# One stride per load of x, a first chunk reordered, and the tables split 17 and 10: a change to the head of a fused FFT and channel-mix kernel

## The chip, the cores and the metric

The kernel runs on one core of a Trainium2 chip. The metric is the time on the device in microseconds (us). The kernel before took 457.84 us (median of three runs, 457.7 to 458.09). A profile shows a "span" that is about 1.8 us shorter than the time of the same run. A difference of less than 2% counts as "same"; this whole study is about tenths of a per cent, so most comparisons were timed in five rounds beside the kernel before on the same chip. A gain or a loss against the kernel before is spoken of where the 95% interval of the ratio leaves out 1.

## The reference

```python
X = np.fft.fft(x, axis=1); X = np.fft.fft(X, axis=2); x = X.real   # x: (8, 3072, 256)
x_prev = concat([zeros, x[:, :-1]], axis=1)
xk = mu_k * x + (1 - mu_k) * x_prev
xr = mu_r * x + (1 - mu_r) * x_prev
k = np.maximum(xk @ w_k, 0)          # 256 -> 1024
v = k * k @ w_v                      # 1024 -> 256
r = 1 / (1 + np.exp(-(xr @ w_r)))    # 256 -> 256
return r * v
```

So each of the 8 batches goes through a two-dimensional Fourier transform (real part) and then through three projections with a squared relu and a sigmoid gate.

## The kernel before

The transform is done by matmuls in stages: `a_sum` or `a_item` (48 points along the sequence, on 96 partitions), `d_item` (along the model dimension, into `g_all`), `c_item` (64 points along the sequence, with tables `m1` and `m2` of 27 "slots", into `pq`). Then VectorE forms halves, differences and mixes, and TensorE does the projections of 48 chunks, in a list of steps. Each step has one `k_piece` (a quarter of a chunk's first projection), one `v_tile` of an earlier chunk, and whatever is registered for that step with `at`. The results of matmuls stand in PSUM, and ScalarE (ACT) or VectorE (DVE) copies them out, which is called evacuating. A gather is a DMA on GpSimd (POOL) that fetches rows by a list of indices; x is the input and `mu` the mixing weights. The parts that matter here:

```python
def load_part(b, h, n, q0, nq):            # x of one batch, on two times 48 partitions
    for g in range(2):
        r0 = 32 * g + 16 * h + q0
        nc.gpsimd.dma_start(out=xh_t[b, h][48 * g:48 * g + 48, q0:q0 + nq],
                            in_=x_r[b, :, r0:r0 + nq, :])
...
NS1 = 9                                    # slots in the first part of the tables
...
def loads():                               # all issued on GpSimd
    ...                                    # gathers of wk[0], mu
    load_xh(1, 0)
    ...                                    # gathers of wr[0], load of wv
    load_xh(1, 1)
    ...                                    # gathers of wk[1], wr[1]: not needed before step 12
...
def mirrored_mu():                         # mu for the mirrored half, first used at step 8
    for a in range(2):
        V.tensor_copy(out=mu_m[:, a], in_=mu_f[:, 1 - a])
    V.tensor_copy(out=mu_m[0:1], in_=mu_f[0:1])
...
at(0, m_rest, 1)                           # special slots 25 and 26, on VectorE
at(5, plain_128)                           # tables for the later batches, on VectorE
at(7, mirrored_mu)
at(8, mix, 0, 0, 1, 0)                     # reads mu_m
```

Of the kernel before, what the change touches and what calls it, by code (L numbers as in the profile page):

```python
# [35 lines left out]
def kernel(  # L36
# [14 lines left out]
    P = 128  # L51
# [3 lines left out]
    NS1 = 9  # L55
# [42 lines left out]
    x_r = x.rearrange("b (n1 r) d -> b n1 r d", r=R)  # L98
# [3 lines left out]
    def load_part(b, h, n, q0, nq):  # L102

        for g in range(2):
            r0 = 32 * g + 16 * h + q0
            nc.gpsimd.dma_start(out=xh_t[b, h][48 * g:48 * g + 48, q0:q0 + nq],  # L106
                                in_=x_r[b, :, r0:r0 + nq, :])

    def load_xh(b, h):
        xh_t[b, h] = xh_pool.tile([96, 16, 256], FP16, name="xh")  # L110
        load_part(b, h, 1, 0, 16)
# [36 lines left out]
    load_part(0, 0, 2, 0, 8)  # L148
# [4 lines left out]
    load_part(0, 0, 2, 8, 8)  # L153
# [5 lines left out]
    load_part(0, 1, 2, 0, 8)  # L159
    load_part(0, 1, 2, 8, 4)  # L160
    load_part(0, 1, 2, 12, 4)
# [21 lines left out]
    def g_zeros(u0, u1):  # L183
# [8 lines left out]
    hi48 = const.tile([P, 1], FP32)  # L192
# [14 lines left out]
    V.tensor_scalar(out=hi48, in0=pcol_f, scalar1=48.0, scalar2=None, op0=ALU.is_ge)  # L207
    V.tensor_scalar(out=n1f, in0=hi48, scalar1=-48.0, scalar2=pcol_f,
# [4 lines left out]
                    scalar2=1.0 / N1, op0=ALU.mult, op1=ALU.mult)  # L213
# [6 lines left out]
    for g in range(2):  # L220
        for n in range(2):
            V.tensor_scalar(out=w_sg[:, n, g:g + 1], in0=hi48, scalar1=2.0 * g - 1.0,
                            scalar2=1.0 - g, op0=ALU.mult, op1=ALU.add)
        V.tensor_scalar(out=w_sg[:, 2, g:g + 1], in0=hi48, scalar1=1.0 - 2.0 * g,
                        scalar2=g - 1.0, op0=ALU.mult, op1=ALU.add)
# [72 lines left out]
    def m_rest(part):  # L298



        s = 26 if part else 0
        if part:
            V.tensor_scalar(out=m2[hi64, 25], in0=m1[hi64, 25], scalar1=-1.0, scalar2=None,
                            op0=ALU.mult)
            V.tensor_copy(out=m1[hi64, 25], in_=m1[lo64, 25])
        for n, m in enumerate((m1, m2)):
            V.tensor_scalar(out=m[hi64, s], in0=m[hi64, s], scalar1=-1.0, scalar2=None,
                            op0=ALU.mult)
            if part:  # L310
                V.memset(m[lo64, 25], 0.0)
            else:
                V.tensor_copy(out=mz[lo64, n], in_=m[lo64, 1])
                V.memset(m[:, 0, 0:1], 0.0)
# [11 lines left out]

    g_zeros(13, 24)
# [8 lines left out]
    def loads():  # L336

        V.memset(mu_f, 0.0)
        mus = [mu.rearrange("(a b) -> a b", b=1) for mu in (moe_mu_k, moe_mu_r)]
        for i, mu in enumerate(mus):  # L340
            nc.sync.dma_start(out=mu_f[0:1, 0, i:i + 1], in_=mu[0:1])
            nc.sync.dma_start(out=mu_f[1:65, 0, i:i + 1], in_=mu[1:129:2][0:64])
            nc.sync.dma_start(out=mu_f[65:128, 0, i:i + 1], in_=mu[2:128:2])
        for a in range(2):
            gather(wk_sb[0][a], moe_w_k, a)
        for i, mu in enumerate(mus):
            gather(mu_f[:, 1, i:i + 1], mu, 1)
        load_xh(1, 0)
        for a in range(2):
            gather(wr_sb[0][a], moe_w_r, a)  # L350
        nc.gpsimd.dma_start(out=wv_sb, in_=moe_w_v.rearrange("(fc p) v -> p fc v", p=128))
        load_xh(1, 1)
        for a in range(2):
            gather(wk_sb[1][a], moe_w_k, 2 + a)
        for a in range(2):
            gather(wr_sb[1][a], moe_w_r, 2 + a)
# [12 lines left out]
    def plain_128():  # L369

        V.memset(w_eo[:, 0, 63:64], 1.0)
        V.tensor_scalar(out=w_eo[:, 0, 127:128], in0=w_eo[:, 0, 127:128], scalar1=-2.0,
                        scalar2=1.0, op0=ALU.mult, op1=ALU.add)
        V.memset(u128, 0.0)

        V.tensor_copy(out=tw[lo64, 0, 1:NSL], in_=m1[lo64, 1:NSL, 0])
        V.tensor_copy(out=tw[hi64, 0, 1:NSL], in_=m2[hi64, 1:NSL, 0])
        V.tensor_copy(out=tw[hi64, 1, 1:NSL], in_=m1[hi64, 1:NSL, 0])
        V.tensor_scalar(out=tw[lo64, 1, 1:NSL], in0=m2[lo64, 1:NSL, 0], scalar1=-1.0,
                        scalar2=None, op0=ALU.mult)  # L380
        V.memset(tw[hi64, :, 1:2], 0.0)

        for n, half, sign in ((0, lo64, 1.0), (0, hi64, -1.0), (1, lo64, -1.0), (1, hi64, 1.0)):
            V.tensor_scalar(out=tw[half, n, 0:1], in0=tw[half, n, 2:3], scalar1=sign,
                            scalar2=None, op0=ALU.mult)
# [55 lines left out]
    def d_half(b, u, ps, eng):  # L441
        d_units(b, ps, u, 2)
        evac(g_all[:, u:u + 2, 1:257],
             ps[:, 0:512].rearrange("p (i c) -> p i c", c=256), eng)

# [81 lines left out]
    def mix_short(b, lo, hi):  # L527

        x_t[b, 0, 0] = xo = x_t.get((b, 0, 0)) or mix_pool.tile([P, 2, 1536], FP16, name="x00")
        for a in range(2):  # L530
            V.scalar_tensor_tensor(out=xo[:, a, 64 * lo:64 * hi],
                                   in0=_v(x_t[b], 64 * (26 * a + lo), [(1, 64 * (hi - lo))]),
                                   scalar=mu_f[:, a, 0:1],
                                   in1=_v(y_t[b], 64 * (NSL * a + lo), [(1, 64 * (hi - lo))]),
                                   op0=ALU.mult, op1=ALU.add)
# [4 lines left out]

    def mix2(b, j, m, lo, hi):
        for a in range(2):
            mix(b, j, m, a, lo, hi)
# [41 lines left out]
    def v_tile(c, tb):  # L585

        apart = c == chunks[-1] and tb >= 2
        h = 0 if apart else tb % 2
        if h == 0:
            st["v"] = ps_v()  # L590
        for fc in range(8):
            nc.tensor.matmul(out=st["v"][:, 256 * h:256 * h + 256],  # L592
                             lhsT=k2_t[c][:, fc, 128 * tb:128 * tb + 128],
                             rhs=wv_sb[:, fc], start=(fc == 0), stop=(fc == 7))

    def v_out(c, tb, n):
# [6 lines left out]
                               in0=st["v"][:, 0:256 * n], scalar=16.0,  # L603
# [17 lines left out]
    m_rest(0)  # L621
    loads()
    m_angles(NS1, NSL)
# [8 lines left out]
    m_wrap(NS1, NSL)  # L632
# [7 lines left out]
    d_item(0, 2)  # L640
    m_sine(NS1, NSL)
    d_item(0, 3)
    for lo, hi in ((0, 4), (4, 8)):
        halves(0, lo + (lo > 0), hi + 1)
        diff(0, lo, hi)
        mix_short(0, lo, hi)
# [5 lines left out]
    def at(step, f, *args):  # L652
        work.setdefault((step, "x" if f in (a_item, a_sum, d_item, c_item, r_item) else "w"),
                        []).append((f, args))

    def mirrored_mu():

        for a in range(2):
            V.tensor_copy(out=mu_m[:, a], in_=mu_f[:, 1 - a])
        V.tensor_copy(out=mu_m[0:1], in_=mu_f[0:1])  # L660

    chunks = [(b, m, i) for b in range(B) for m in range(2) for i in range(3)]
    nk = 4 * len(chunks)
    LAG = 5
    keep_busy(4)
    k_products(chunks[0], 0, 0, 256)
    k_products(chunks[0], 1, 0, 256)
    d_half(0, 16, ps_v(), "A")
    d_half(0, 18, ps_v(), "A")
    for n, c in enumerate(chunks):  # L670
        at(4 * n + (5 if n in (0, 2) else 4), r_item, c)


    at(0, m_swap, NS1, NSL)
    at(0, m_rest, 1)
    at(0, mix2, 0, 1, 0, 0, 8)
    at(1, c_item, 0, 9, 8)
    at(1, halves, 0, 9, 17)
    at(1, diff, 0, 8, 16)
    at(1, mix2, 0, 0, 0, 8, 16)  # L680
    at(2, d_item, 0, 5)
    at(2, a_sum, 1, 0, 0)
    at(3, c_item, 0, 17, 8)
    at(5, butterfly, 1, 1, 0)
    at(4, halves, 0, 17, 25)
    at(4, diff, 0, 16, 24)
    at(5, a_sum, 1, 0, 4)
    at(5, a_sum, 1, 0, 8)
    at(5, mix2, 0, 0, 0, 16, 24)
    at(6, a_sum, 1, 0, 12)  # L690
    at(6, c_item, 0, 25, 2)
    at(6, load_xh, 2, 0)
    at(6, mix2, 0, 1, 0, 8, 16)
    at(7, butterfly, 1, 1, 1)
    at(7, halves, 0, 25, 27)
    at(7, diff, 0, 24, 26)
    at(7, mirrored_mu)
    at(7, load_xh, 2, 1)
    at(8, mix, 0, 0, 1, 0)
    at(9, mix, 0, 0, 1, 1)  # L700
    at(10, mix2, 0, 1, 0, 16, 24)
    at(12, mix, 0, 1, 1, 0)
    at(14, mix, 0, 1, 1, 1)
    for n, st0 in enumerate((7, 8, 9, 10)):
        at(st0, a_item, 1, 1, n // 2, n % 2, "A")
    at(5, plain_128)
    for n, st0 in enumerate((12, 13, 13, 14, 15, 17)):
        at(st0, d_item, 1, n)
    at(18, turned, 1)
    for n, st0 in enumerate((14, 15, 18, 19)):  # L710
        at(st0, c_item, 1, (0, 7, 14, 21)[n], 7 if n < 3 else 6)

    for b in range(B):
# [8 lines left out]
        if t < B:  # L722
            for n, st0 in enumerate((9, 10, 12, 14) if b else (11, 13, 15, 24)):
# [9 lines left out]
        if t < B:  # L733
            at(s0 + 16, halves, t, 0, 14)
# [13 lines left out]
    for step in range(nk + LAG):  # L748
# [3 lines left out]
        vs = step - LAG  # L752
        if vs >= 0:
            v_tile(chunks[vs // 4], vs % 4)
        due(step, "w")
        if vs >= nk - 2:
            v_out(chunks[vs // 4], vs % 4, 1)
        elif vs >= 0 and vs % 2:
            v_out(chunks[vs // 4], vs % 4, 2)
# [34 lines left out]
```

## Time and profile before

The profile that the prediction quotes further down was of a run of 461.26 us. In a timeline of TensorE (PE) the columns are start, busy time, engine, line, operation, output from inputs, shape, count, and in brackets the idle time before the group with what ended it.

```profile
9.46 1.48 PE L421 MATMUL psW<-w_pm,xh 96*128 96x192 f16 x16 [1.44 <-DMA xh<-in_x_dram]
...
19.43 0.27 PE L555 MATMUL psW<-x,wk 128*128 128x256 f16 x1
19.88 0.92 PE L555 MATMUL psW<-x,wk 128*128 128x256 f16 x7 [0.17 <-DVE x L531]
...
25.08 0.82 PE L421 MATMUL psW<-w_pm,xh 96*128 96x192 f16 x8 [0.31 <-ACT pq L395]
...
28.54 1.67 PE L555 MATMUL psW<-x,wk 128*128 128x512 f16 x7 [0.33 <-DVE x L523]
...
33.77 1.02 PE L555 MATMUL psW<-x,wk 128*128 128x512 f16 x4 [0.49 <-ACT r L583]
```

The reader is to see one large wait (1.44 us, for x) and, after the first projection at 19.43, only small ones: 0.17, 0.31, 0.33 and 0.49.

| kernel before | trace the prediction used | second trace |
|---|---|---|
| time of the profiled run, us | 461.26 | 457.92 |
| span, us | 459.5 | 456.1 |
| first projection starts, us | 20.52 | 19.43 |
| PE busy of 10 us, 20 to 30 | 6.66 | 9.10 |
| bracketed PE waits, first projection to 40 us | 3.71 | 1.30 |
| PE time lost in the head, counted as the prediction counts it, us | 5.6 | 3.3 |

### The profile page before, as it was taken

What the parts mean: (1) busy time and instruction counts of PE and PEld (TensorE: products, weight loads), DVE (VectorE), ACT (ScalarE), POOL (GpSimd) and SP (SyncE); (2) the same over time, 40 slices, a digit from 0 to 9 for tenths busy, and PEclk for the clock granted to TensorE, in tenths of its full rate; (3) what the DMA queues carried; (4) which work ended last, traced back from release to release, by engine and by line L of the source; (5) the groups of instructions that cost most, each with busy time, mean ns of one, the idle gap of its engine ahead of it and who ended that gap; (6) DMA issues with size and microseconds to landing.
All of it is one profiled execution on the core that took longest, in us unless ns stands there. A gap on an engine that the chain in (4) does not pass through costs nothing.

```text
span 459.5 us, 9804 instructions
## 1 busy us (share of the span) xinstructions
PE 447.2 (97%) x4087; PEld 327.6 (71%) x4087; DVE 360.0 (78%) x532; ACT 358.8 (78%) x398; POOL 35.6 (8%) x67
## 2 busy tenths in 40 slices
PE   8879999999999999999999999999999999999996
PEld 4647777777777777777777777777777777676764
DVE  7779988987788877978698777888679855898453
ACT  4689898888877887888887888878887888666661
POOL 8831000000000000000000000000000000000000
PEclk9999999999999999999999999999999999999999
DMA  7894561626622274214722265212222221223223
GB/s 131 128 177 90 120 140 46 124 64 138 124 62 67 49 146 109 70 48 90 164 68 58 59 136 120 69 48 69 55 63 61 56 70 47 71 64 75 70 68 93
DMA packets 32972, 40.25 MB, mean 88 GB/s; under 512 B 4480, under 2 KB 30592, under 8 KB 31584
## 3 DMA queue, kind: packets, MB, share of 16 engines
q1 hardware_dynamic: 28080, 25.07, 21.9%
q0 software_dynamic: 4688, 14.42, 18.8%
q8 instruction: 32, 0.52, 0.5%
q10 hardware_dynamic: 160, 0.13, 0.1%
q14 instruction: 12, 0.10, 0.1%
HBM read 28.84 MB, written 25.17 MB: 118 GB/s over the span
## 4 chain that ended last, share of the span: by engine, by line
PE 93%; ACT 3%; DMA 1%; POOL 1%; issue 1%; DVE 0%; another core or an unknown queue 0%; POOLq 0%
PE psV L592 36%; PE psW L555 35%; PE psW L578 9%; PE psW L431 5%; PE psW L407 4%; PE psW L458 3%; DMA xh<-in_x_dram 1%; ACT rl L565 1%; ACT g_all L395 1%; PE psW L421 1%; POOL xh L106 1%; ACT a L395 0%; ACT L583 0%; ACT pq L395 0%; ACT m L287 0%
## 5 line engine op out<-in xcount | busy, mean ns | idle before, releaser
L565 ACT ACTIVATE rl<-psW 128x1024 f16<-128x1024 f32 x192 | 196.7, 1026 | 80.8 <-PE psW L555 80.4
L555 PE MATMUL psW<-x,wk 128*128 128x512 f16 (+1 forms) x776 | 197.4, 377 | 2.5 <-ACT rl L565 1.5
L592 PE MATMUL psV<-wv_sb,k 128*128 128x256 f16 x1536 | 198.6, 272 | 0.0
L571 DVE TENSOR_TENSOR k<-rl 128x2048 f16<-128x2048 f16 x96 | 117.4, 1224 | 62.5 <-ACT rl L565 61.8
L592 PEld LDWEIGHTS <-k 128*128 128x128 f16 x1536 | 143.7, 98 | 20.3
L555 PEld LDWEIGHTS <-wk 128*128 128x128 f16 x776 | 75.7, 98 | 53.3 <-issue 4.0
L602 DVE SCALAR_TENSOR_TENSOR o<-psV,r 128x512 f32<-128x512 f32 (+1 forms) x97 | 66.3, 684 | 22.9 <-PE psV L592 20.7
L523 DVE TENSOR_TENSOR x<-y,t 128x1536 f16<-128x1536 f16 (+1 forms) x70 | 61.8, 882 | 2.4
L395 ACT ACTIVATE a<-psW 128x768 f16<-128x768 f32 x62 | 49.6, 806 | 4.0 <-PE psW L421 2.1
L578 PE MATMUL psW<-wr,x 128*128 128x256 f16 x384 | 49.8, 273 | 0.0
L583 ACT ACTIVATE r<-psW 128x1024 f16<-128x1024 f32 x48 | 49.0, 1021 | 0.8 <-PE psW L578 0.8
L578 PEld LDWEIGHTS <-x 128*128 128x128 f16 x384 | 37.6, 98 | 14.4 <-issue 0.2
L395 ACT ACTIVATE g_all<-psW 128x1024 f16<-128x1024 f32 (+1 forms) x46 | 46.9, 1022 | 1.1 <-PE psW L431 1.1
L106 POOL DMA_DIRECT2D xh<-in_x_dram x38 | 19.7, 525 | 238.7 <-DVE eo L119 222.7
L431 PEld LDWEIGHTS <-a 128*128 128x128 f16 x384 | 25.1, 98 | 10.0 <-issue 0.2
L407 PEld LDWEIGHTS <-eo 96*128 96x128 f16 x416 | 23.4, 97 | 11.6
L119 DVE TENSOR_TENSOR eo<-xh 96x2048 f16<-96x2048 f16 x26 | 31.5, 1213 | 0.0
L395 ACT ACTIVATE pq<-psW 128x896 f16<-128x896 f32 (+5 forms) x33 | 28.7, 871 | 1.6 <-PE psW L431 1.1
L431 PE MATMUL psW<-w_eo,a 128*128 128x128 f16 x368 | 27.7, 219 | 0.0
L407 PE MATMUL psW<-w_pm,eo 96*128 96x96 f16 x416 | 26.3, 205 | 0.0
L458 PEld LDWEIGHTS <-g_all 128*128 128x128 f16 x459 | 17.8, 98 | 7.7 <-issue 0.7
L510 DVE TENSOR_SCALAR t<-d,mu_f 128x1536 f16<-128x1536 f16 (+1 forms) x38 | 20.6, 543 | 0.1
(106 smaller groups left out, 158.5 us busy)
## 6 DMA issues: line engine op xcount, KB each, us to landing
out_dram<-o SPq DMA_DIRECT2D x190, 128.0 KB
xh<-in_x_dram POOLq DMA_DIRECT2D x28, 384.0 KB
xh<-in_x_dram POOLq DMA_DIRECT2D x6, 192.0 KB
wv_sb<-in_moe_w_v_dram POOLq DMA_DIRECT2D x1, 512.0 KB
xh<-in_x_dram POOLq DMA_DIRECT2D x4, 96.0 KB
out_dram<-o ACTq DMA_DIRECT2D x2, 64.0 KB
out_dram<-o SPq DMA_DIRECT2D x2, 64.0 KB
y<-f SPq DMA_DIRECT2D x7, 3.4 KB
```

The lines of the kernel that those rows point to most:

```text
L395: nc.scalar.activation(out=out_ap, in_=in_ap, func=AF.Copy)
L407: nc.tensor.matmul(out=ps[:, 128 * i:128 * i + 96], lhsT=eo[:, 8 * j + i, e, :], rhs=w_pm[0:96, 0], start=True, stop=True)
L431: nc.tensor.matmul(out=_v(ps, 256 * i + 64 * (1 - e), [(128, 2), (1, 64)]), lhsT=a_t[b][:, e, 2 * u:2 * u + 2, :], rhs=w_eo[:, e, :], star ...
L458: nc.tensor.matmul(out=ps[:, o + 64 * i:o + 64 * i + 64], lhsT=g_all[:, u, col:col + 128], rhs=m[:, sl] if sl != 1 else mz[:, 0 if m is m1 ...
L523: V.tensor_tensor(out=dst, in0=_v(y_t[b], 64 * (NSL * a + lo + 3 * m), [(1, n)]), in1=_v(x_t["t", a], 64 * lo, [(1, n)]), op=ALU.subtract ...
L555: nc.tensor.matmul(out=st["k", ds][:, 512 * hs + lo:512 * hs + hi], lhsT=wk_sb[m][a][:, 128 * fc:128 * fc + 128], rhs=xk[:, a, 512 * i + l ...
L565: nc.scalar.activation(out=st["rl"][:, 2 * ds:2 * ds + 2], in_=st["k", ds].rearrange("p (f t) -> p f t", f=2), func=AF.Relu, bias=0.0, sca ...
L571: V.tensor_tensor(out=k2_t[c][:, 2 * ds - 2:2 * ds + 2], in0=r, in1=r, op=ALU.mult)
L578: nc.tensor.matmul(out=ps[:, 256 * tb:256 * tb + 256], lhsT=x_t[b, 1, m][:, a, 512 * i + 128 * tb: 512 * i + 128 * tb + 128], rhs=wr_sb[m] ...
L583: nc.scalar.activation(out=st["r", c], in_=ps, func=AF.Sigmoid)
L592: nc.tensor.matmul(out=st["v"][:, 256 * h:256 * h + 256], lhsT=k2_t[c][:, fc, 128 * tb:128 * tb + 128], rhs=wv_sb[:, fc], start=(fc == 0), ...
L602: V.scalar_tensor_tensor(out=o.rearrange("p a b -> p (a b)")[:, 0:256 * n], in0=st["v"][:, 0:256 * n], scalar=16.0, in1=st["r", c][:, 256 ...
```

## The change

The author's intent: fewer and simpler loads of x, so that x comes sooner; a first part of the tables large enough for the first chunk, so that its second sine is out of the way; the first chunk reordered (slots 9 to 16 before the second quarter of its projection, its v tiles one step sooner, its r product one step later) so that TensorE has work while ScalarE evacuates; and small table work moved from VectorE, which is nearly full in the head, to GpSimd, which has little to do from about 28 us on. The core of the diff (the sign tables' adaption to the new partition order, `m_rest` split in two, and most `at` lines are cut):

```diff
-    NS1 = 9
+    NS1 = 17
-    x_r = x.rearrange("b (n1 r) d -> b n1 r d", r=R)
+    x_r = x.rearrange("b (p r) d -> b p r d", r=32)
-    def load_part(b, h, n, q0, nq):
-        for g in range(2):
-            r0 = 32 * g + 16 * h + q0
-            nc.gpsimd.dma_start(out=xh_t[b, h][48 * g:48 * g + 48, q0:q0 + nq],
-                                in_=x_r[b, :, r0:r0 + nq, :])
+    def load_part(b, h, q0, nq):
+        nc.gpsimd.dma_start(out=xh_t[b, h][:, q0:q0 + nq],
+                            in_=x_r[b, :, 16 * h + q0:16 * h + q0 + nq, :])
 ...
+        nc.gpsimd.dma_start(out=wv_sb, in_=moe_w_v...)     # moved up, before load_xh(1, 0)
 ...
-            V.tensor_copy(out=mu_m[:, a], in_=mu_f[:, 1 - a])
-        V.tensor_copy(out=mu_m[0:1], in_=mu_f[0:1])
+            nc.gpsimd.tensor_copy(out=mu_m[:, a], in_=mu_f[:, 1 - a])
+        nc.gpsimd.tensor_copy(out=mu_m[0:1], in_=mu_f[0:1])
 ...                                     # plain_128 and the last special slots likewise
+    v_steps = {4 * n + tb + (LAG if n else LAG - 1): (c, tb) ...}
 ...
-    at(0, m_rest, 1)
-    at(5, plain_128)
-    at(7, mirrored_mu)
-    at(8, mix, 0, 0, 1, 0)
+    at(1, m_last)                        # GpSimd
+    at(5, plain_128)                     # GpSimd
+    at(5, mirrored_mu)                   # GpSimd
+    at(9, mix, 0, 0, 1, 0)
```

The number of matmuls stays the same (4087 records in both profiles).

## The prediction

> **What bounds the kernel now.** I read the page first, then the table of windows, then the timeline of TensorE (PE) over the first 60 us, and last those of ScalarE (ACT), VectorE (DVE) and GpSimd (POOL).
>
> ```profile
> PE 447.2 (97%) x4087; PEld 327.6 (71%) x4087; DVE 360.0 (78%) x532; ACT 358.8 (78%) x398; POOL 35.6 (8%) x67
> PE 93%; ACT 3%; DMA 1%; POOL 1%; issue 1%; DVE 0%; another core or an unknown queue 0%; POOLq 0%
> ```
>
> PE is busy 97% of the span, and 93% of the chain that ended last is PE. Only about 12 us have no PE work in them. The windows tell where (columns: PE, PEld, DVE, ACT, POOL busy, clock, DMA share, GB/s):
>
> ```profile
> 10.00:20.00 10.00, 7.45 (x99) 5.87 (x98) 7.57 (x25) 5.85 (x10) 8.31 (x10) 1.00 0.78 118
> 20.00:30.00 10.00, 6.66 (x71) 4.49 (x70) 7.44 (x23) 8.18 (x10) 6.65 (x8) 1.00 1.13 178
> 30.00:40.00 10.00, 9.26 (x95) 6.65 (x93) 9.65 (x27) 9.97 (x12) 0.59 (x2) 1.00 0.47 84
> 40.00:50.00 10.00, 10.00 (x94) 7.23 (x92) 9.79 (x20) 8.49 (x11) 1.51 (x3) 1.00 0.94 174
> 150.00:200.00 50.00, 50.00 (x470) 36.97 (x469) 40.59 (x51) 41.36 (x47) 2.02 (x4) 1.00 0.42 91
> ```
>
> From 40 us on PE is full to the end of the batch loop; before that it is not. So there are two regimes: a head of 40 us, in which a chain of loads, table building and evacuations sets the pace, and 420 us bound by PE. The change keeps the matmul count (same number of PE instructions in both programs) and reorders only the head, up to about step 20. What it can win is the time that PE loses in the head. The timeline of PE shows the lossy part:
>
> ```profile
> 11.80 2.14 PE L421 MATMUL psW<-w_pm,xh 96*128 96x192 f16 x24 [1.29 <-DMA xh<-in_x_dram]
> ...
> 20.52 1.46 PE L555 MATMUL psW<-x,wk 128*128 128x256 f16 x8
> 21.81 0.61 PE L431 MATMUL psV<-w_eo,a 128*128 128x128 f16 x8
> 22.26 1.26 PE L555 MATMUL psW<-x,wk 128*128 128x256 f16 x8
> 23.43 0.96 PE L458 MATMUL psW<-m,g_all 128*128 128x64 f16 x24
> 25.31 1.02 PE L555 MATMUL psW<-x,wk 128*128 128x512 f16 x4 [0.92 <-ACT rl L565]
> 26.23 0.61 PE L431 MATMUL psW<-w_eo,a 128*128 128x128 f16 x8
> 28.37 0.82 PE L421 MATMUL psW<-w_pm,xh 96*128 96x192 f16 x8 [1.53 <-issue]
> 29.80 1.02 PE L555 MATMUL psW<-x,wk 128*128 128x512 f16 x4 [0.62 <-ACT rl L565]
> ...
> 37.43 1.02 PE L555 MATMUL psW<-x,wk 128*128 128x512 f16 x4 [0.64 <-ACT r L583]
> ```
>
> The reader should see three things: PE waits for x at 11.8; the first projection (L555) starts at 20.52; between it and 40 PE idles four times for ACT (the 1.53 under "issue" ends as ACT's evacuation of pq, begun at 27.29, ends at 28.31, and that frees the PSUM buffer).
>
> The bracketed gaps understate the loss, because the modelled end of a group lies about 0.2 us past its last issue. I count by pitch instead, from the full stretch: 8 matmuls of 256 columns 0.88, 4 of 512 0.87, 8 of 192 0.66, 8 of L431 0.45, 24 of L458 0.69, 8 of L407 0.34. Between 20.52 and 45.03 PE issued 9 projection pieces (7.8), 4 v tiles (3.5), two r items (1.8), four pieces of the next batch's first stage (2.6), two L431 groups (0.9), 54 of L458 (1.6), two of L407 (0.7): 18.9 us of work in 24.5. So **5.6 us are lost there**, and 1.3 at the x load.
>
> **What the Trainium skill says.** (1) Perfetto Trace Analysis, Identifying the Most-Contended Engine: matmul busy share is a poor measure of distance to roofline, weight-load share a better one. The trace agrees: PE stands at 10.00 of 10 from 40 us, weight loads at 37 of 50. (2) DMA: Bandwidth & Descriptors, Rules for kernel authors: two transfers to disjoint partition halves serialize, use one. Before, each load of x is such a pair, issued in 0.50 to 0.67 us each; the DMA share is near 1 from 4 us to 11, so halves bring no bandwidth here. (3) GPSIMD Engine Reference, Engine selection: one-input elementwise work runs near line rate there. In the trace its one-column operations take 0.19 to 0.40 us against 0.15 on DVE: slower, but nothing urgent waits. (4) SBUF — State Buffer, Who interferes with whom: DVE in a two-port mode and GpSimd block each other. No row of this trace isolates that; it is a risk for the work moved to POOL.
>
> **Part by part.**
>
> *x on 96 partitions, one stride.* Ten issues in the head become five. POOL's first x issue is at 1.24, its last ends at 7.48; six issues of 0.5 us stand at 4.43 to 7.48. Five at 0.55 (estimate: 96 rows cost little more than 48, as the 1.00 us of the weight load with 1024 rows suggests) with the short iotas behind them end near 5. DMA is then limited by bytes: x of batch 0 is 1.57 MB in SBUF, moved at about 200 GB/s when full, some 8 us from 2.3, so about 10.7 for the end instead of 12. The load waited for at 11.66 should land near 11. In steady state POOL and DMA are hidden: worth nothing there.
>
> *Tables of 17 and 10 slots.* The first angle sum goes from 576 to 1088 elements: 0.76 to 1.27 us (the 1152 form takes 1.34), the wrap 0.46 to 0.72, the sine 0.78 to 1.19, the two swaps 0.31 to 0.45 each. About 1.3 us more in front, given back as the 11-unit zeroing (0.8) moves behind and the second part shrinks. By adding durations DVE reaches its first evacuation at 13.1 (before 13.31) and ends the last at 15.0 (before 15.29). So DVE lets only about 0.35 of the faster load through: first projection at 20.2. What the 17 slots buy: slots 9 to 16 no longer need the second sine, which stood at 21.22 in ACT between two evacuations, nor its swap at 22.57.
>
> *Order of the first chunk.* Slots 9 to 16 are transformed before the second half of piece 1, and chunk 0's four relus follow each other instead of having pq, g_all and a in between. By hand, in the new order, with durations above: slots 9 to 16 end at 22.4 (waiting for two evacuations), piece 1 at 23.8, piece 2 waits for the first relu (0.95), piece 3 ends 26.4, chunk 1 starts 26.8 (before 31.4). The v tiles come a step earlier: the first waits about 1.1 for its second squaring (DVE 28.5 to 29.7), then they fill PE. Piece 0 of chunk 2 ends at 40.9. Before it ends at 42.94, and PE has by then also done 0.5 of L458 and L407; by 45.03 also an r item and another L407. Subtracting all that work (1.73) from 45.03 gives 43.3 for the same state: **gain 2.4 us**. Check: 5.6 lost before, about 3.2 lost now, 0.35 earlier start.
>
> *Work moved to POOL* (second half of the special slots 1.15 us, the twiddle setup 1.6, mirrored mu 0.4): about 3.1 us off DVE in 22 to 45, where it is 96 to 98% busy. The fused mixes are about even (0.71 estimated against 0.35 + 0.42). This is no gain by itself, but DVE must keep up with a PE that is 2.4 us ahead, and this gives it the room.
>
> *wv before the next x.* The v tiles now need it at 28.5, before at 35.75; issued near 15 rather than 20.67 it should land by 21.
>
> From 40 us PE is full in both, so the gain passes to the end unchanged. I take 0.1 off: **455.5 us**.
>
> **Rivals.** (a) *The faster load is all that counts, or nothing of it*: if DVE kept up, another 1 us; if the 17-slot sine holds back ACT's evacuations (its four end at 10.96, now 11.8), the 0.35 is lost: 456.0 or so. (b) *ACT becomes the bound of the head.* It is 9.97 of 10 busy at 30 to 40 us and its list is the same length, so PE can only gain what ACT idled (1.11 at 26.2, 0.41 at 28.3, 0.9 at 19.4). I cannot explain the first two: those matmuls had ended long before by the modelled times. If such late starts recur at the new places, 1 to 2 us go: 457. (c) *DVE or POOL late*: a blocked POOL delays the special slots or the twiddles past step 8 or 18, PE waits in 45 to 60: up to 459. (d) *The v tiles fill all holes*: 5 us gained, 453. A gain over 2% would need 9.2 us, more than the 6.9 lost in the head.
>
> **Range and chances.** (b) and (a) pull up, (d) down: 453.0 to 457.2 at 8 in 10. Faster by over 2%: 0.02; within 2%: 0.97; slower: 0.01.
>
> **What would show it.** Right: x waits of PE near 11 us shorter by 0.5 or more; first projection at 20.0 to 20.4; chunk 1's first piece near 27; first v tile near 29; PE at 10 of 10 from about 38; the window 100 to 400 unchanged. Wrong: PE gaps in 40 to 60, first projection later than 20.5 (17 slots too dear), a v tile waiting for wv, or a POOL row that a mix waits for.

## The result, and the profile after

The changed kernel took 458.02 us (median of four runs, 457.93 to 458.12), the kernel before in the same rounds 457.92 (457.7 to 458.09). The ratio is 1.0002, with a 95% interval from 0.9985 to 1.002. Ratios and intervals are those over the fast runs of both kernels; they are not quite the ratios of the medians quoted. The predicted class, "same", came out, which says little, as it had 0.97 and needed no mechanism; the predicted time, 455.5, did not, and 458.02 lies outside the range of 453.0 to 457.2.

The page of the changed kernel, first the busy times, then the shares of the chain that ended last:

```profile
PE 446.3 (98%) x4087; PEld 326.7 (72%) x4087; DVE 356.8 (78%) x501; ACT 358.4 (79%) x398; POOL 36.2 (8%) x69
PE 89%; POOL 4%; DVE 3%; DMA 2%; issue 1%; ACT 0%; POOLq 0%
```

GpSimd (POOL) has 4% of the chain, 3% in the second trace of before (the kernel before profiled again, in a run of 457.92 us, with its timeline of PE above); new in its share are the moved operations on `m` and `tw`, 1% each. The windows (same columns as in the prediction) of the stretch from 40 to 50 us, before (second trace) and then after:

```profile
40.00:50.00 10.00, 9.98 (x95) 7.30 (x94) 9.79 (x20) 7.88 (x10) 1.00 (x2) 1.00 0.76 159
```

```profile
40.00:50.00 10.00, 8.66 (x85) 6.30 (x84) 7.94 (x13) 7.44 (x9) 3.70 (x12) 1.00 0.62 119
```

PE falls from 9.98 to 8.66 of 10, and VectorE (DVE) from 9.79 to 7.94. The head had been faster until then. Timeline of PE of the changed kernel:

```profile
18.26 0.83 PE L556 MATMUL psW<-x,wk 128*128 128x256 f16 x4
...
25.82 0.61 PE L593 MATMUL psV<-wv_sb,k 128*128 128x256 f16 x4 [0.19 <-DVE k L572]
...
47.47 0.81 PE L556 MATMUL psW<-x,wk 128*128 128x512 f16 x3 [1.34 <-DVE x L525]
```

The first projection starts at 18.26, 1.17 us sooner than in the second trace of before, and no matmul waits for x any more. But at 47.47 PE waits 1.34 us for a mix. That mix was late because of what VectorE waited for just before (timeline of DVE, changed kernel):

```profile
43.15 0.62 DVE L512 TENSOR_SCALAR t<-d,mu_m 128x1536 f16<-128x1536 f16 x1 [1.96 <-POOL mu_m L658]
```

And the mirrored mu was late because of what GpSimd had in front of it (timeline of POOL, changed kernel):

```profile
24.27 1.05 POOL L330 DMA_INDIRECT wr<-in_moe_w_r_dram,row_i  x1 [0.30 <-issue]
32.95 3.16 POOL L313 TENSOR_SCALAR m<-m 64x64 f16<-64x64 f16 x4 [7.63 <-DVE x L536]
...
37.87 3.23 POOL L378 TENSOR_SCALAR tw<-m 64x26 f16<-64x26 f16 x4
...
41.32 1.06 POOL L382 TENSOR_SCALAR tw<-tw 64x1 f16<-64x1 f16 x4
42.44 0.43 POOL L657 COPY mu_m<-mu_f 128x2 f32<-128x2 f32 x2
```

GpSimd issues its last gather by 25.3 and then stands still for 7.63 us. The timeline names a VectorE mix as the releaser, but in the raw records an event wait for the semaphores of gathers stands just before this row, from 25.30 to 32.66, and one of the two is that of the gather issued at 24.27. Then ten microseconds of small operations follow in order, and the mirrored mu, three tiny copies that need none of them, comes last at 43.1. VectorE had been ready for it at 41.2.

**Theory A:** the loads of x win about 1.2 to 1.7 us in the head, and the wait for the mirrored mu, itself caused by GpSimd's order behind late gathers, gives them back. **Rival B:** the gap at 47 is only where a general lateness shows; the reorder and the 17 slots cost what the loads win, and moving mu changes nothing. **Rival C:** the wait on GpSimd is for VectorE, as the timeline says, not for the gathers. A second question is which part of the change carries the gain.

### The profile page after: what moved, and what is told of

Its sections match the earlier page's. It is cut to its first block, busy times and chain, and to the rows that moved or that the text cites. A ratio compares the mean times of both kernels' runs of the same rounds, so it can differ in the third digit from the quotient of the medians.

```text
span 456.1 us, 9765 instructions
## 1 busy us (share of the span) xinstructions
PE 446.3 (98%) x4087; PEld 326.7 (72%) x4087; DVE 356.8 (78%) x501; ACT 358.4 (79%) x398; POOL 36.2 (8%) x69
## 4 chain that ended last, share of the span: by engine, by line
PE 89%; POOL 4%; DVE 3%; DMA 2%; issue 1%; ACT 0%; POOLq 0%
PE psV L593 35%; PE psW L556 34%; PE psW L579 9%; PE psW L429 4%; PE psW L405 4%; PE psW L460 2%; DMA wr<-in_moe_w_r_dram,row_i 2%; POOL wr L330 1%; POOL tw L378 1%; POOL m L313 1%; POOL wk L330 0%; DVE x L525 0%; POOL mu_f L330 0%; DVE g_all L182 0%; DVE rl L278 0%
## 5 line engine op out<-in xcount | busy, mean ns | idle before, releaser
L525 DVE TENSOR_TENSOR x<-y,t 128x1536 f16<-128x1536 f16 x60 | 57.5, 959 | 2.1
L104 POOL DMA_DIRECT2D xh<-in_x_dram x19 | 10.4, 550 | 225.6 <-DVE eo L117 224.5
L492 DVE TENSOR_TENSOR y<-pq 128x896 f16<-128x896 f16 (+5 forms) x38 | 18.7, 532 | 3.4 <-ACT pq L393 3.4
```

The costliest lines, as they stand in the source:

```text
L525: V.tensor_tensor(out=dst, in0=_v(y_t[b], 64 * (NSL * a + lo + 3 * m), [(1, n)]), in1=_v(x_t["t", a], 64 * lo, [(1, n)]), op=ALU.subtract ...
```

## The experiments

There were eighteen runs of twelve kernels, all correct against the reference. "Before" is the kernel before in the rounds of the same call.

| label | what it is | median us | before | ratio, 95% interval |
|---|---|---|---|---|
| before_again | kernel before, one look | 457.92 | 458.27 | not timed in rounds |
| mu_on_dve | after, mirrored mu on VectorE | 456.39 | 458.27 | 0.9963, 0.9949 to 0.9976 |
| mu_first_on_pool | after, mirrored mu first on GpSimd | 456.40 | 458.27 | 0.9966, 0.9952 to 0.9979 |
| all_on_dve | after, all moved work back on VectorE | 458.86 | 458.27 | 1.0017, 1.0003 to 1.003 |
| before_one_stride | before, loads alone | 456.09 | 457.83 | 0.9962, 0.9948 to 0.9975 |
| before_17 | before, 17 slots alone | 458.62 | 457.83 | 1.0026, 1.0009 to 1.0042 |
| fix_v_late | mu_on_dve, v tiles at the old step | 456.40 | 457.83 | 0.9968, 0.9954 to 0.9981 |
| fix_two_loads | mu_on_dve, each load in two halves | 458.33 | 457.83 | 1.0009, 0.9996 to 1.0023 |
| gathers_late_c | after, late gathers issued last | 456.56 | 457.88 | 0.9971, 0.9954 to 0.9988 |
| before_one_stride_c | as before_one_stride | 456.63 | 457.88 | 0.9971, 0.9954 to 0.9989 |

Eight more runs fell on two disturbed chips and are told at the end of this section.

### The second trace of before, and the mirrored mu moved

before_again is the kernel before, unchanged, profiled anew; its lines stand above. 

> The kernel before, unchanged, profiled again. Its first profiled run took 461.26 us where its unprofiled ones took 457.7 to 458.1, and its trace showed consumers of TensorE starting 0.7 to 2.9 us after the matmuls that they wait for. Theory A (that trace was of an untypical run): this span is near 456, the first projection starts within 0.5 us of 20.5 or earlier, and ScalarE no longer idles 1.1 us at 26 us. Theory B (the head really loses 5.6 us each time): span near 459.5 with the same gaps.

mu_on_dve takes the three copies back to VectorE, at the same step:

```diff
-            nc.gpsimd.tensor_copy(out=mu_m[:, a], in_=mu_f[:, 1 - a])
-        nc.gpsimd.tensor_copy(out=mu_m[0:1], in_=mu_f[0:1])
+            V.tensor_copy(out=mu_m[:, a], in_=mu_f[:, 1 - a])
+        V.tensor_copy(out=mu_m[0:1], in_=mu_f[0:1])
```

> The changed kernel with the three mirrored-mu copies back on VectorE, at the same step. Theory A (what the head wins is given back while VectorE waits 1.96 us at 41 to 43 us for mu_m, the last of ten us of small GpSimd operations, and TensorE 1.34 us at 47): the wait is gone, time 456.3 to 456.8, ratio to the kernel before 0.997. Theory B (the head won nothing and the wait at 47 us is hidden slack): 457.7 to 458.2.

mu_first_on_pool leaves them on GpSimd, but ahead of the special slots:

```diff
+    at(1, mirrored_mu)
     at(1, m_last)
-    at(5, mirrored_mu)
```

> The changed kernel with the three mirrored-mu copies on GpSimd, but issued ahead of the special slots and the twiddles. Theory A (only the place in GpSimd's queue matters): the copies end near 26 us, the wait at 43 us is gone, same time as with the copies on VectorE or 0.1 us less, 456.2 to 456.8. Rival (GpSimd is too slow for these copies wherever they stand): a wait stays, 457.5 to 458.2.

They took 456.39 and 456.40 us, 1.6 less than the changed kernel's 458.02. (It was run at another time. By the ratios to before, 0.9963 against 1.0002, it is 1.8.) The PE gap at 47 is gone in mu_on_dve, and VectorE's multiplication with mu_m starts without a wait, at 41.44 instead of 43.15 (timelines of DVE and PE, mu_on_dve):

```profile
41.44 0.62 DVE L512 TENSOR_SCALAR t<-d,mu_m 128x1536 f16<-128x1536 f16 x1
...
45.68 1.03 PE L556 MATMUL psW<-x,wk 128*128 128x512 f16 x4
```

The timeline of POOL in mu_first_on_pool shows why the second edit works as well:

```profile
24.95 0.31 POOL L657 COPY mu_m<-mu_f 128x2 f32<-128x2 f32 x2
25.32 1.07 POOL L658 COPY mu_m<-mu_f 1x4 f32<-1x4 f32 x1
32.87 3.15 POOL L313 TENSOR_SCALAR m<-m 64x64 f16<-64x64 f16 x4 [6.49 <-DMA wr<-in_moe_w_r_dram,row_i]
```

The copies run right after the last gather is issued, and the special slots still start at 32.87. Nobody else is hurt by that lateness: the time is the same as with mu on VectorE. So the give-back is the mirrored mu's place in GpSimd's order. Rival B falls: 1.6 us come back by moving three copies.

all_on_dve takes all of the moved work back to VectorE (`ts = V.tensor_scalar` and `V.memset` in `m_last` and `plain_128`, and the copies as above):

> The changed kernel with all of the work that it moved to GpSimd (special slots, twiddles, mirrored mu) back on VectorE. If moving it to GpSimd relieves VectorE where it sets the pace, this loses against the version with only mu back: 457 to 458. If VectorE had slack (2.2 us idle at 28 us in the changed kernel), the same, 456.3 to 456.8.

It took 458.86, more than expected. Its timeline of PE:

```profile
26.77 0.61 PE L593 MATMUL psV<-wv_sb,k 128*128 128x256 f16 x4 [1.21 <-DVE k L572]
...
48.31 0.81 PE L556 MATMUL psW<-x,wk 128*128 128x512 f16 x3 [1.05 <-DVE x L525]
```

The special slots on VectorE delay the squares (they start at 25.49, in the changed kernel at 24.54), so the first v tile waits 1.21 us where the changed kernel waits 0.19, and later the mix is late as well. In the new order the move to GpSimd is worth 458.86 less 456.39, some 2.5 us, as long as nothing urgent queues behind it.

### Each part alone

before_one_stride puts only the new loads (the changed `load_part`, its call order and the sign tables that go with it) into the kernel before. 

> The kernel before with the loads of x alone changed (96 partitions, one stride, five issues in front of the long iotas). In the second trace of the kernel before, the TensorE waits 1.44 us for x at 9.46. Theory: that wait is what the change wins in the head (first projection 19.43 -> 18.26 with everything), so the loads alone give about 1.1 us: 456.8 to 457.1, first projection at 18.4 to 18.6. Rival, the prediction's: VectorE and ScalarE reach the first evacuations no earlier, so only some 0.3 us pass: 457.6, first projection at 19.1.

It took 456.09 against 457.83, a gain of 1.74 us where 1.1 was expected. The changed kernel with the mu wait repaired gets the same against its own reference: the ratios are 0.9962 and 0.9963. Timeline of PE:

```profile
18.16 1.23 PE L554 MATMUL psW<-x,wk 128*128 128x256 f16 x8
...
23.67 0.82 PE L420 MATMUL psW<-w_pm,xh 96*128 96x192 f16 x8 [0.31 <-ACT pq L394]
...
27.03 1.67 PE L554 MATMUL psW<-x,wk 128*128 128x512 f16 x7 [0.33 <-DVE x L522]
...
32.26 1.02 PE L554 MATMUL psW<-x,wk 128*128 128x512 f16 x4 [0.49 <-ACT r L582]
```

Compare with the second trace of before: the same three waits of the same lengths, 1.41, 1.51 and 1.51 us sooner. The wait of 1.44 us for x is gone and what stands behind it has moved up by about as much. The loads alone give as much as the whole change does with the wait for mu repaired.

fix_two_loads keeps the new layout and order and splits each load again:

```diff
-            nc.gpsimd.dma_start(out=xh_t[b, h][:, q0:q0 + nq],
-                                in_=x_r[b, :, 16 * h + q0:16 * h + q0 + nq, :])
+        for p in (slice(0, 48), slice(48, 96)):
+            nc.gpsimd.dma_start(out=xh_t[b, h][p, q0:q0 + nq],
+                                in_=x_r[b, p, 16 * h + q0:16 * h + q0 + nq, :])
```

> The changed kernel with the mirrored mu on VectorE (456.39), each load of x split in two of 48 partitions, layout and stride unchanged. If the gain of the loads is the halved number of issues on GpSimd (0.5 us each), x comes later by up to 2 us and the time goes up by 0.7 to 1.3 us: 457.1 to 457.7. If it is the layout or the place of the iotas alone, it stays at 456.3 to 456.6.

It took 458.33, 1.9 us more than the same kernel with whole loads, and more than expected. These are the rows of POOL for the second to the last part of batch 0's x, first in before_one_stride and then in fix_two_loads:

```profile
2.27 2.07 POOL L104 DMA_DIRECT2D xh<-in_x_dram  x4
```

```profile
2.81 4.08 POOL L105 DMA_DIRECT2D xh<-in_x_dram  x8
```

Four issues of 96 rows take 0.52 us each, eight of 48 rows 0.51 each: an issue costs the same for half the rows. PE then waits for x, 1.42 us before the group at 9.50:

```profile
9.50 1.48 PE L420 MATMUL psW<-w_pm,xh 96*128 96x192 f16 x16 [1.42 <-DMA xh<-in_x_dram]
```

So it is the number of transfers, neither the layout nor the place of the iotas. Whether all of it is the time of the issues is not shown. By the raw records the last issue of the second part ends 1.1 us later than in mu_on_dve (3.90 against 2.84), but its last piece lands 1.6 us later (9.37 against 7.76), and the landings are spread more (7.36 to 9.37 for the later half, 7.20 to 7.76 for a whole load). So some 0.5 us arises behind the issues, and no run separates the two.

before_17 sets only `NS1 = 17` in the kernel before. 

> The kernel before with the table parts of 17 and 10 slots alone. Theory: worth nothing without the earlier x and the reorder; the longer first angle sum, wrap and sine (about 1.3 us on VectorE, 0.4 on ScalarE) stand in front of the evacuations, the shorter second part saves the same later: 457.6 to 458.2. Rival: the second sine between two evacuations of the first chunk was a cost on the path, so 17 slots alone win 0.5 or more: 457.4 or less. Third: the longer front delays the first projection by 0.4 or more and nothing comes back: 458.3 or more.

It took 458.62, 0.8 us more than before by medians. Its first projection starts at 19.32, no later than in before; the loss shows further on, where PE waits 0.44 us at 39.93 for a mix on VectorE, where the same group in before loses only about 0.3 (8 matmuls from 39.28 to 40.46, where the next r product takes 0.87):

```profile
39.93 0.94 PE L578 MATMUL psW<-wr,x 128*128 128x256 f16 x7 [0.44 <-DVE x L523]
```

That explains a part of the 0.8; the rest stays open, and none of the three expectations fits. By the numbers the 17 slots alone are a small loss in the old order, not the even exchange that I had worked out.

fix_v_late is mu_on_dve with the first chunk's v tiles back at the old step (`v_steps = {4 * n + tb + LAG: ...}`). 

> The changed kernel with the mirrored mu on VectorE (456.39) and the first chunk's v tiles back at the old step (5 behind, as all others); its r product stays two steps late. In the trace of the changed kernel the early v tile waits 0.19 and 0.52 us for the squares. Theory: the early step is not where the gain comes from: within 0.4 us of 456.39, with those two gaps gone and perhaps another one for ScalarE in their place. Rival, the prediction's: the early v tiles fill holes while ScalarE's relus are awaited, so taking them away costs 0.7 us or more: 457.1 or above.

It took 456.40 against 456.39. The two waits for squares (0.19 and 0.52) are gone and two others, 0.44 and 0.42 for ScalarE, have come in. The earlier v tiles gain nothing.

### Is it the gathers that GpSimd waits for?

gathers_late is the changed kernel with the last four gathers issued behind the mirrored mu, which stays on GpSimd at its place:

```diff
         load_xh(1, 1)
-        ...gathers of wk[1], wr[1]
+    def gathers_1():
+        ...gathers of wk[1], wr[1]
 ...
     at(5, mirrored_mu)
+    at(5, gathers_1)
```

> The changed kernel with one edit: the four gathers of the second half's weights (wk, wr) are issued behind the mirrored mu instead of in front of the special slots; mu stays on GpSimd at its old place. In the trace of the changed kernel the first special-slot operation on GpSimd starts at 32.95, 7.6 us after GpSimd's last issue; an event wait just before it lists the transfers of the gathers. Theory: it waits for those gathers to land, so now it starts by 27 to 29, the mirrored mu is done by 38 to 40, before VectorE asks for it at 41.2, and the time is 456.2 to 456.6 with no gap on TensorE near 47. Rival: it waits for VectorE's swap or sine (the releaser that the timeline names), starts near 33 as before, and the time stays at 458.0.

Its first two runs fell on disturbed chips; the third, gathers_late_c, was on an undisturbed one, beside the loads alone. 

> The same kernel as gathers_late. On an undisturbed chip: 456.2 to 456.6 if the wait for the late gathers is the whole give-back, 457.5 to 458.0 if not. On a disturbed one: near 459.9 again, like before_one_stride_c within 0.5 if the disturbance is the chip's.

> The same kernel as before_one_stride. On an undisturbed chip (kernel before near 457.9): 456.0 to 456.3 again. On a disturbed one (kernel before near 459.4): if the disturbance is the chip's and hits every kernel with an early x, the gain of 1.7 shrinks or turns: 459 to 460, with a granted clock of 0.5 for some us before 25; if it belongs to the edits sent there, the gain stays: 457.5 to 457.9.

gathers_late_c took 456.56, before_one_stride_c 456.63, the kernel before 457.88. Timeline of POOL in gathers_late_c:

```profile
25.53 2.97 POOL L313 TENSOR_SCALAR m<-m 64x64 f16<-64x64 f16 x4 [5.88 <-ACT g_all L395]
...
35.33 0.60 POOL L660 COPY mu_m<-mu_f 1x4 f32<-1x4 f32 x1
36.09 1.04 POOL L330 DMA_INDIRECT wk<-in_moe_w_k_dram,row_i  x1 [0.16 <-issue]
```

The special slots start at 25.53 instead of 32.95, the mirrored mu is done at 35.9 instead of 43.1, VectorE's multiplication with it starts at 41.28 without a wait, and PE has no bracketed wait after 34.4 in the head. VectorE's work was not moved at all. So rival C falls: with those four gathers out of the way the operation starts 7.4 us sooner. Why the compiled instruction waits for transfers whose data it doesn't read is left open; the first special-slot operation carries these waits, the mirrored copies in mu_first_on_pool don't.

### On two chips the head runs differently

Eight runs fell on two chips on which the kernel before itself took 459.6 and 459.2 us. The kernel before was timed there but not profiled. All eight are below; their times don't decide between the theories.

| label | edit | median us | before |
|---|---|---|---|
| gathers_late, gathers_late_b | as above | 459.95, 459.87 | 459.6, 459.2 |
| one_stride_17, one_stride_17_b | before_one_stride with `NS1 = 17` | 461.78, 459.63 | 459.6, 459.2 |
| one_stride_pool, one_stride_pool_b | before_one_stride with `m_last`, `plain_128`, `mirrored_mu` on GpSimd at the old steps | 460.12, 460.39 | 459.6, 459.2 |
| fix_9, fix_9_b | mu_on_dve with `NS1 = 9` and the second swap behind its sine | 466.13, 465.24 | 459.6, 459.2 |

> The kernel before with the one-stride loads and the table parts of 17 and 10 slots, no reorder. The loads alone gave 456.09, the 17 slots alone cost 0.8 (458.62 against 457.83). If the cost of the 17 slots (a longer front on VectorE and ScalarE) was hidden behind the late x before and shows in full now: 456.8 to 457.1. If it was a clash with the late x and goes away with the early one: 456.0 to 456.3.

> The kernel before with the one-stride loads (456.09) and the special slots, the twiddle setup and the mirrored mu on GpSimd, at their old steps. Theory: GpSimd's order alone gives the gain back, without the reorder: the mirrored mu comes at 42 to 43.5 instead of 40.2 while VectorE wants it at 41.2, so 1 to 2 us go: 457.1 to 458.0. Rival: without the reorder VectorE has room in its order and the relief of some 3 us balances it: 455.8 to 456.4.

> The changed kernel with the mirrored mu on VectorE (456.39) and table parts of 9 and 18 slots as before, the second part's swap placed right behind its sine (slots 9 to 16 need it). If 17 slots cost something with the early x too, this is faster: 455.6 to 456.1, the best so far. If the sine and swap in front of slots 9 to 16 hold back the first chunk as the change's author meant, it is slower: 456.7 or more.

> The same kernel as gathers_late (the four late gathers issued behind the mirrored mu), on a chip that is hopefully undisturbed. The first trace showed the special slots starting at 27.84 and the mirrored mu done at 39.0, ahead of VectorE's request. If that wait is the whole give-back: 456.2 to 456.6, as with mu moved (456.39, 456.40). If the mu was only a sign of something else: 457.5 to 458.0.

> The same kernel as one_stride_17. Full cost of the 17 slots with the early x: 456.8 to 457.1. No cost with the early x: 456.0 to 456.3. The first projection against 18.16 of the loads alone shows where it comes from.

> The same kernel as one_stride_pool. GpSimd's order alone gives the gain back: 457.1 to 458.0, with VectorE waiting for mu_m near 41 to 43 and a gap on TensorE after it. The relief of VectorE balances it: 455.8 to 456.4.

> The same kernel as fix_9 (changed kernel, mu on VectorE, parts of 9 and 18 slots). The disturbed run showed VectorE 4 us late for the first projection, which no clock explains by itself. If 9 slots hold the new order back, it is slower than 456.39 on a good chip too: 457 or more, the first projection later than 18.2. If that was the chip alone: 455.6 to 456.4.

The windows of gathers_late_b show the clearest case (the third number from the end is the granted clock: 0.83, then 0.51):

```profile
13.00:16.00 3.00, 0.00 (x0) 0.00 (x0) 0.89 (x4) 1.30 (x2) 2.70 (x4) 0.83 0.74 108
16.00:22.00 6.00, 5.96 (x63) 5.27 (x63) 4.25 (x10) 3.35 (x5) 2.97 (x4) 0.51 1.11 173
```

First the results of the last matmuls on x come late: the semaphore updates of matmuls that had ended by 12.77 in the modelled times stand at 14.04 and 15.5. PE has nothing to do for 3.27 us meanwhile, and from 15.0, still within that gap, its clock reads half for nearly seven microseconds. The same gathers_late on an undisturbed chip (456.56) has neither. The Trainium skill, page TensorE: Matmul & The Clock Gate, section HAM oscillation, says that idle gaps of more than about 3.4 us drop the clock to half. The drop is here, but these traces do not bear out the length: one_stride_pool_b has it at 14.78 in a gap of 2.39 us,

```profile
15.29 1.01 PE L140 MATMUL psV<-zeros 128*128 128x512 f16 x2 [2.39 <-ACT a L403]
```

and gathers_late at 15.72 between gaps of 2.00 and 1.02. Nor is the clock the whole loss: one_stride_17_b shows no drop and still took 459.63, and two runs of gathers_late_b with a mean clock of 1.0 took 459.86 and 459.88. What makes the results late on these chips no run settles; a clock record that is itself off is not excluded. The trace that the prediction used shows late results too (0.7 to 2.9 us), without a drop; whether it has the same cause is not shown. before_one_stride_c was meant to meet such a chip and didn't, so it stays open whether the loads' gain survives there. The two runs of fix_9 show one thing beside the chip: PE waits 4.15 and 4.27 us for VectorE's first mixes, because I had put the second swap in front of them. That is my edit's fault, so fix_9 tells nothing about 9 slots against 17. What the 17 slots cost with the early x, and whether GpSimd's order alone would give the gain back in the old order, stay open.

Five edits beat both kernels on undisturbed chips, by 0.3 to 0.4%: the loads alone (456.09 and 456.63), and the changed kernel with mu moved to VectorE (456.39, and 456.40 with the v tiles late) or to the front of GpSimd's list (456.40), or with the late gathers behind it (456.56). Their ratios to before do not differ beyond their intervals.

## Why the prediction was wrong, point by point

- **PE bounds the kernel, and what the head gains passes to the end.** Right as a mechanism: the loads alone gain 1.3 to 1.5 us up to 34 us and 1.74 at the end. "From 40 us PE is full in both" was wrong for the changed kernel: 8.66 of 10 in 40 to 50.
- **"5.6 us are lost there".** Mis-sized, because the trace was of an untypical run. The prediction noted two late starts that it could not explain and put them in a rival; they were the sign. By the same count the second trace loses 3.3. So the 2.4 that the reorder was to win are about the excess of the one trace, and they were taken off 457.84, the median of runs without that excess. The time of the profiled run, 461.26, against that median could have told it before anything else.
- **The loads of x.** The prediction had the x that PE waited for landing near 11 and VectorE letting 0.35 us of it through. By the raw records that part landed at 9.85 (11.66 in the first trace). The changed head needs no wait for x at all, and the first projection starts at 18.26 (predicted 20.0 to 20.4; the typical run before, 19.43). VectorE let more through: its first evacuation came at 12.30, not 13.1, and its last ended at 13.95, not 15.0. This term was worth about 1.7 us and was sized at 0.35.
- **17 slots, "about even".** Alone they cost 0.8 us. With the early x it is open.
- **The reorder, "gain 2.4 us".** This is the term that was mis-sized most, through its base and not through its picture of the new order. Counted the same way, mu_on_dve loses 3.0 us from 18.18 to 43.60, where the prediction said about 3.2; only the 5.6 before is 3.3. (Its check does not add up either: 5.6 less 3.2, plus 0.35 for the earlier start, is 2.75 and not 2.4.) The new head also ran sooner than drawn: chunk 1 starts at 24.16, not near 27. With the mu wait repaired the changed kernel stands at 0.9963 of before, the loads alone at 0.9962: reorder, 17 slots and the move to GpSimd together add nothing that can be measured; without the move they lose the gain of the loads again (458.86). The early v tiles by themselves: 456.39 against 456.40.
- **Work moved to GpSimd, "slower, but nothing urgent waits".** This is the step whose failure set the result. The mirrored mu is urgent, and it stood behind a wait of 7.35 us for gathers and ten microseconds of small operations. It cost 1.6 us; without it (456.39) the time would have been inside the range, but by luck, as the terms for loads and reorder err by about 1.4 and 2.4 in opposite directions. The other half of the sentence held: VectorE needed the room, by 2.5 us.
- **The rivals.** Rival (c), DVE or POOL late and PE waiting in 45 to 60, up to 459, is what happened, and "a POOL row that a mix waits for" was on the list of signs. It was given too little weight: the prediction looked at the durations of the moved operations and not at what they queue behind.

In one sum: loads -1.7, reorder with 17 slots and GpSimd's relief about 0, wait for the mirrored mu +1.6 to +1.8, so 458.02 against 457.92.

## What to carry to other kernels

Before sizing gaps in a trace, check that the profiled run is a usual one: compare its time with the median of the runs. When work moves to an idle engine, draw that engine's whole queue, issues of transfers and the waits they bring included, and ask of each moved result who needs it first; put the urgent ones ahead. And count the transfers on a path, not only the bytes: half as many for the same bytes was the whole gain here.

## What the Trainium skill lacked or had wrong

- DMA: Bandwidth & Descriptors, Rules for kernel authors, advises one transfer in place of two to disjoint partition halves because the two share the same engines. The runs agree with the advice but show another cost, which the section doesn't give: each issue on GpSimd took 0.51 to 0.52 us whether for 48 or 96 rows, and splitting cost 1.9 us of the kernel's time (458.33 against 456.39). The same page's Anatomy of one DMA calls descriptor generation "small, variable" and puts no figure to it; eight issues in a row held GpSimd for 4.08 us here.
- GPSIMD Engine Reference, Engine selection, gives one-input work as roughly line rate. For small operations that is no guide: the four special-slot operations of 64x64 took 3.16 us on GpSimd (changed kernel) and 0.81 on VectorE (all_on_dve). How much of the 3.16 is waiting for VectorE no run separates.
- SBUF — State Buffer, Who interferes with whom, has GpSimd and some kinds of VectorE instructions block each other on a shared port. No run isolates it. In line with it, one and the same one-column operation on GpSimd took 1.17 us in the changed kernel and 0.19 in mu_first_on_pool.
- No page that I read says that a GpSimd operation can be compiled to wait for indirect gathers issued earlier on the same engine; here that wait was 7.35 us (start at 32.95 against 25.53 with the gathers moved).
- TensorE: Matmul & The Clock Gate, HAM oscillation, puts the drop of the clock behind idle gaps of more than about 3.4 us. Here the record fell to 0.5 in shorter ones: 2.39 us in one_stride_pool_b, 2.00 and 1.02 in gathers_late (by modelled ends of matmuls). I found no page that says why matmul results came up to 2.7 us behind their modelled ends on some chips.
